# Crossbar transposes for two of four batches in a fused attention and gated-convolution kernel, with other first biases, smaller mask work and another instruction order

## The chip, the cores and the metric

One core of a Trainium2 chip runs the whole program. The metric is the device time of one execution in microseconds (us). The engines are called as in the profile: PE (matrix multiply), DVE (vector), ACT (scalar), POOL (GpSimd) and SP, which here only issues DMAs. PE writes its results to eight PSUM banks; DVE and ACT move them on to SBUF, the on-chip memory. All transfers, from whichever engine they are issued, run on the core's 16 DMA engines.

## The reference

Four batches, eight heads, 768 positions, head size 64. Each position attends to the 95 before it, itself and the first eight ("global") keys, with a penalty that grows with distance by a slope for each head. The attention output, 768 x 512 for each batch, goes through a gated long convolution:

```python
scores = scale * np.matmul(q, k.transpose(0, 1, 3, 2)) + bias      # bias = -slope * distance
a = softmax(np.where(keep, scores, -1e9))
x = np.matmul(a, v)                                  # to (batch, 768, 512)
x1, x2, x3 = np.split(x @ w_proj, 3, axis=-1)
x2_conv = np.fft.irfft(np.fft.rfft(x2, axis=1) * np.fft.rfft(filter_fft, axis=0), axis=1)
out = (x1 * x2_conv * x3) @ w_out
```

Inputs and output are float32; inside the kernel nearly everything is float16, with float32 sums in PSUM.

## The kernel before

**Attention** (`attention`, L855). Positions are taken in seven tiles of 120 keys, each with the eight global keys in front (128 rows), in three groups c0, c1, c2 of two, two and three tiles. For a group, q and k must stand transposed, head size on the partitions (`QT`, `KT`). There are three ways: `turned32` (L628) transposes float32 rows on PE, for the first tiles of batch 0, which SP loads as they are; `turned` (L665) transposes float16 tiles on PE, 4 matmuls of 128 columns a tile, and a copy on ACT or DVE moves them from PSUM; `crossed` (L651) has SP issue a DMA that transposes from SBUF to SBUF, without PE. The list `XB = (3,)` says that batch 3 goes the third way. Then, for each pair of heads hp and each group, `scores` (L685) multiplies k by q, ACT takes the exponential (L721), and DVE multiplies by a mask (L738), which holds the exponential of the distance bias and the zeros.

In batch 0 the masks are not ready in time, so there the bias is added on PE before the exponential: `slope` (a diagonal of the slope, in two halves of 64 rows) times `near` (the distances in two halves), L698, 96 matmuls in all. `near` and `slope` are written by ACT and DVE in `distances` (L477); `masks` (L535) spreads the distances into a row of 648 columns and takes eight exponentials of it on ACT, before batch 0's attention in the order of the program.

`values` (L741) multiplies the weights by v, divides by the sums (L780 on DVE, L784 on ACT), and leaves the attention output `xn` with positions on the partitions. `transpose_x` (L790) turns it on PE (L801) and ACT or DVE copies it to `xT` (L303), packed without gaps: 768 columns for each of four blocks of 128 features.

**Convolution** (`conv`, L891). `butterfly` (L808) adds and subtracts the two halves of `xT` on DVE; `gate` (L830) multiplies `xT` by the first and last third of the weights in two halves of 384 positions (L840) and multiplies the two results (L851); the projection (L909), the forward transform (L621), the product with the filter's spectrum (L1072 to L1078), the inverse transform (L934, L937) and the mixing on DVE follow, and `y` times the last weights gives the output rows (L961), six blocks of 128 a batch, stored by SP (L969) from a ring of six buffers `ot`. `tables` (L409) and `spectrum` (L549) make the transform's sines and the filter's spectrum once.

**The order.** `ORDER` (L39) is a list written out in the program: each word is an operation's number, the engine that runs it, and for PE the PSUM banks, as in `87P0`. Numbers count the operations in the order in which the program makes them. A word such as `i14b0` stands for 14 matmuls without use, which only keep PE busy. Each engine runs its operations in this order, so whichever is late holds up all behind it on its engine. Loads are issued by POOL (L319), which also converts to float16; SP issues the first float32 tiles, the copies of the global rows (`kn<-kn`, `vn<-vn`), the crossings and the stores. The costs in the program (`act`, `dve`, `pe`) were used to make such an order and do not run on the chip.

Of the kernel before, what the change touches and what calls it, by code (L numbers as in the profile page):

```python
# [26 lines left out]
def act(n):  # L27
    return 0.06 + n / 1200.0
# [11 lines left out]
5G 33V 34A 1V 16S 0V 12V 20S 4V 41A 43A 9V 8V 39A 10A 44A 36A 6A 49A 48A 19S 37A 45A 24G 17S 18S 50G 55G 25V 11V 26G  # L40
13V 56G 40A 42A 7V i14b0 87P0 54G 28A 53G 60G 31A 85P1 61G 59G 27A 72V 62G 52G 35A 81P2 51G 57G 46A 58G 83P3 47A 88A
29V 30V 32V 90P0 63G 89A 86A 82V 38A 91V 84A 21V 114P2 115V 94P01 98P45 116P2 78A 65G 99A 64G 15V 117V 95A 92P67 112P3
113V 93A 110P2 96P45 97A 158P3 66G 111V 122P01 123A 120P67 121A 22V 68G 159V 3G 160P3 161V 14V 23S 156P2 118P45 162P3
67G 119A 124P01 261G 157V 163V 164P23 125A 166P45 100P01 165A 101V 102V 167A 105P67 170P23 171A 69G 168P01 169A 131P45
262G 263G 106V 107V 108P2 132V 133V 260G 126P67 127V 76A 103P3 104A 109V 128V 75A 134P4 221P5 74A 135V 172P01 73A 173V
259G 129P6 216P4 177P23 79A 130V 136P6 174V 175P7 178V 70G 146P0 217A 264S 179V 180P1 137P2 222A 223V 142P3 176A 218V
219V 71G 80A 271G 202V 181A 183P1 182P4 203V 220A 224V 209V 144A 141P5 210V 138A 211V 148V 205V 361P3 273G 225A 139V
140V 272G 270G 265S 188P7 185A 362A 212V 213V 151P6 266G 363P3 2A 153V 143A 364V 359P2 360V 152P6 228P3 154V 276G
365P01 190A 184V 77A 204V 279G 366A 206V 207V 371P45 198P2 277G 226V 367V 155V 297P7 368P01 214V 372A 373V 215V 208V
200A 374P45 187P6 278G 229A 274G 145V 491G 298A 288P2 375A 269G 275G 369A 289A 488G 286P7 227V 235V 236V 189V 237V  # L50
147P4 149V 238V 287A 150V 230A 231A 232A 233V 284P2 285A 312P7 292P6 313A 293A 389P5 387P2 192P7 390A 194A 193P6 195A
388V 394P45 395A 400P01 234V 391P23 392A 239V 240V 376V 299P7 300A 437P6 401A 301P4 302A 282G 268S 433P5 435P7 438V
281G 370V 397P23 398A 241V 249P6 250A 393V 434V 247P4 436V 402V 267S 382P01 494S 242P5 248A 448P67 243A 439P23 493S
440A 383V 384V 449A 396V 303P4 377P01 197P5 199A 304A 399V 408P23 441V 492G 244P6 378V 379V 305P5 409V 410V 380P4
445P01 245A 442P23 280G 381V 306A 196V 446A 450V 403P67 404V 443A 411P5 489G 587P4 499G 405V 256P01 412A 490G 385P6
257A 505G 386A 258A 591P7 588V 252P45 253A 254A 507G 406P0 447V 456P23 661P1 444V 508G 501G 662A 407V 414P0 589P4 590A
251V 307V 416A 310P5 311A 511G 290P6 424P1 457V 458V 291A 426A 459P0 423P4 425A 429P6 308V 431A 500G 451P23 665P1
418P6 255V 592A 191V 615P4 314V 315V 506G 718G 309V 322P7 452V 246A 460A 502G 420A 453V 186V 323A 617P5 719G 454P0
455A 295V 294V 296V 732G 666V 318P6 721S 413P7 616A 330P0 316P2 509G 481V 482V 484V 317A 326P1 618A 415A 663P4 428P2
201V 430V 319A 320P3 321V 324P5 483V 325A 331V 328P7 327A 419P6 329A 421V 422V 495G 472P2 730G 664A 283G 734G 466P7  # L60
432V 476P3 474A 497S 468A 599P45 735G 628P01 478V 600A 498G 529P2 332V 629A 485V 486V 530A 462P3 676P45 677A 333V 601V
673P01 674A 596P67 487V 516P2 597A 334V 464A 512P4 726G 513A 527P5 602P67 517V 717G 593P23 603A 630V 728G 619P01 620A
525P4 675V 514P6 528V 335V 336V 339V 504G 526A 622P01 496S 594A 625P45 626A 340V 477P7 621V 623A 479A 627V 598V 515A
503G 737G 427V 467P2 469A 350P3 670P01 739G 624V 667P45 671A 540P7 541A 604V 353P6 722S 716G 533P2 668A 733G 595V 337V
461P0 354A 520P7 470V 531P1 605P45 417V 606V 521A 729G 351A 818S 538P6 607V 534A 356P7 539A 817S 636P45 338V 463A 637V
532A 638V 631P23 632V 357A 633A 518P0 471P1 639P7 640A 519A 672V 473A 669V 678V 341P6 342A 888S 610P45 608P2 344P3
345A 542V 611V 612V 510G 684P45 890S 609V 480V 613P2 634P6 614A 536V 465V 523V 679P01 635A 685V 686A 347P7 535V 646P6
652P2 654A 656P3 731G 843S 680V 681V 543V 648A 682P4 736G 658A 475V 687P5 688A 651P2 815S 522V 524V 653A 544P3 552P6
545A 537V 720G 816S 819S 823P01 824A 683V 553A 709V 710V 723G 724S 725S 712V 829P45 554P3 711V 713V 555A 647P2 830A
738G 714V 657P0 659A 548P3 549A 556P6 715V 546P1 547A 845S 660V 558P4 559A 649A 557V 704P0 706V 550P1 348A 551A 642P3  # L70
644A 560V 561V 690P2 692A 844S 727G 842S 562V 849P67 852P01 846P45 641P3 563V 564V 740P2 853A 753P0 847A 741V 826P45
850A 643A 855P67 820P23 754A 827A 744P1 891S 831V 567V 565V 699P0 821A 757P4 745A 568V 742P1 856A 655V 758A 566V 889S
854V 895P67 701A 768P4 743A 755P5 857V 746P1 352S 756V 896A 769A 747A 748P0 645V 355S 898P67 828V 901P45 892P23 575P1
825V 899A 749A 851V 650V 902A 848V 705P6 707A 822V 897V 689P0 900V 837P45 349S 838V 839V 893A 751V 700P6 702A 576A
695P7 697A 858P23 859V 860V 832P45 894V 766P1 767A 691A 759P7 761P6 762A 903V 578P1 750V 343S 752V 840P6 833V 863P23
864V 865V 760A 694P7 834V 579A 909P01 910V 911V 841A 346S 770V 904P23 861P6 862A 866P4 771V 572P5 573A 835P6 569P0
836A 912P5 905V 906V 584P6 763V 570A 764V 765V 867A 772P0 773A 907P4 784P1 908A 913V 934V 935V 780P2 778P0 696A 779A
781A 884P3 774P7 786P0 580S 936V 886A 708V 787A 937V 782P2 938V 358S 585V 581P3 785A 577S 776P1 775A 883P7 777A 783A
788V 958P0 959V 939V 940V 879P2 941P6 698V 586S 942V 789A 790V 885A 873P0 791V 881A 954P1 955A 875A 956P2 693V 967P1
969P6 957A 945P0 868P2 703V 930P7 968A 870A 943P1 960P2 962P4 869P5 792V 795V 796V 944A 961A 812P2 793V 970A 794V 946A  # L80
947P6 871A 574S 963A 971V 972V 887V 949P5 878P4 813A 950A 948A 874P2 876A 582A 803P5 964V 965V 966V 992P2 979P6 952V
951V 988P3 583S 975P0 980A 877V 800P1 953V 990P6 976A 880V 993A 804V 986P2 801V 991V 987A 989A 814S 994V 872V 977P4
978A 882V 973P5 974A 981V 995A 571S 996V 997V 982V 983V 984V 915P0 985V 809P6 797P1 810A 920P6 922A 998V 798A 999V
811S 1000V 1001V 919P5 932A 929P4 806P1 1012V 799S 917A 914P0 1002V 807A 808S 925P7 921A 923V 931A 933V 916V 927A 805S
918V 1013V 924P5 1009P4 926A 802S 1003P5 1004A 1005S 1014V 1010A 1011S 1006P0 1007A 1008S 928V 1015V 1019P5 1020A
1021S 1022P4 1023A 1016P5 1024S 1017A 1018S
# [112 lines left out]
class Fused:  # L199
    PERIOD = 40.0  # L200
    NEAR = 3
# [6 lines left out]
    XB = (3,)  # L208
# [26 lines left out]
    def buffers(self):  # L235
# [14 lines left out]
        self.xT = t("xT", [P, 4, S])  # L250
# [20 lines left out]
        self.x1p = t("x1", [P, 4, S // 2])  # L271
# [6 lines left out]
        self.dg = t("dg", [P, 264], BF16)  # L278
        self.far = t("far", [NG, 216])
        spare = self.eo.rearrange("p a b c -> p (a b c)")  # L280
        self.near = spare[:, 0:960].bitcast(BF16).rearrange("p (a b) -> p a b", a=2)
        self.slope = spare[:, 960:1984].bitcast(BF16).rearrange("p (a b c) -> p a b c", a=4, b=2)
        self.idle = t("idle", [P, 512])
        self.ident = t("ident", [P, P])
        self.ident32 = self.p3.bitcast(F32).rearrange("p a b -> p (a b)")[:, 256:384]
        self.warm = t("warm", [1, 2], F32)
        self.row = spare[0:1, 1984:2624].rearrange("p (a b) -> p a b", a=5)
        self.wide_dg = self.mix.bitcast(BF16).rearrange("p a b c -> p (a b c)")[:, 0:648]
# [76 lines left out]
    def setup(self):  # L365
# [12 lines left out]

        def rows(_):
# [10 lines left out]
        g.op("V", dve(512, 2), lambda _: v.memset(self.ot[3][0:NG], 0.0), w=[("kz", 0)], bias=-4500)  # L390
        for lo, hi in ((1, 2), (2, 7)):
            g.op("V", dve(512 * (hi - lo), 4), lambda _, lo=lo, hi=hi: v.memset(self.kn[0:NG, lo:hi], 0.0),
                 w=[("kz", t) for t in range(lo, hi)], bias=-4500 if lo == 1 else -3500)
# [15 lines left out]
    def tables(self):  # L409
# [3 lines left out]
        for a, n in enumerate((512, 256)):  # L413
# [16 lines left out]
            e, self.twin.rearrange("p s a (b c) -> p (s a) b c", b=2),  # L430
            self.fwd[:, 4:6].rearrange("p s (a c) -> p (s a) c", a=2)[:, :, None].to_broadcast([P, 4, 2, 64])),
            r=[("fwd", 1)], w=["twin"], name="twin")
        g.op("V", dve(256, 4), lambda _: nc.vector.tensor_scalar(
            self.fwd[:, 6:8], self.fwd[:, 1:4:2], -1.0, None, op0=Alu.mult), r=[("fwd", 0)],
            w=[("fwd", 2)])

# [787 lines left out]
```

## Time and profile before

| | us |
|---|---|
| three timed runs | 179.90, 180.12, 178.73 (median 179.9) |
| span of the profiled execution | 176.2 (no other time of this execution is shown) |
| busy: PE, DVE, ACT, POOL | 163.8, 156.3, 148.7, 78.2 |
| last matmul ends, last store issued | 172.5, 173.6 |
| first exponential, first crossing | 12.45, 82.9 |

A busy time is the part of the span in which an engine has at least one instruction under way. Matmuls overlap, so a full PE is not PE at its peak; in the chain of work that ended last each matmul has only the time by which it moved the end. `bank<-xT,w` is the tile written and the tiles read; L840 is the line, and for helpers such as `copy` (L303), `times` (L307, L309) and `load` (L319) it is that of the helper. The granted clock of TensorE is 1.00 in all stages.

### The profile page before, as it was taken

How to read it: one execution, taken by the hardware profiler on the slowest of the kernel's cores; microseconds unless marked ns; L12 is line 12 of the kernel's file. 1: busy time of each engine (PE TensorE's matmuls, PEld its weight loads, DVE VectorE, ACT ScalarE, POOL GpSimd, SP SyncE). 2: the span in 40 equal slices, each digit the busy share in tenths (PEclk: the TensorE clock that was granted, in tenths of full speed). 3: DMA queues.
4: the chain of work that ended last, by engine and by line, in shares of the span. 5: the costliest groups of instructions: out<-in, count | busy, mean ns of one | idle time of the engine just before them, and what ended most of it. 6: DMA issues, size and time to landing. Idle time of an engine off the chain costs nothing.

```text
span 176.2 us, 4332 instructions
## 1 busy us (share of the span) xinstructions
PE 163.8 (93%) x1662; PEld 100.3 (57%) x1662; DVE 156.3 (89%) x339; ACT 148.7 (84%) x294; POOL 78.2 (44%) x99
## 2 busy tenths in 40 slices
PE   5989999689999999999899999999999999989981
PEld 2547976354655767654356767444676644556530
DVE  7685569869999999999999999999999999999960
ACT  6999998949999988889989999899856855957852
POOL 7999998828999468799950000000000000000000
PEclk9999999999999999999999999999999999999999
DMA  4999999999999989999999995400031030041564
GB/s 110 184 149 140 142 173 170 196 193 154 159 155 159 149 53 106 156 167 155 130 161 169 131 96 159 179 4 0 0 118 65 0 125 0 0 180 40 192 242 186
DMA packets 98188, 22.23 MB, mean 126 GB/s; under 512 B 90879, under 2 KB 95095, under 8 KB 98167
## 3 DMA queue, kind: packets, MB, share of 16 engines
q0 software_dynamic: 82992, 12.41, 98.6%
q1 hardware_dynamic: 15175, 9.54, 23.1%
q8 instruction: 13, 0.21, 0.5%
q14 instruction: 8, 0.07, 0.1%
HBM read 25.84 MB, written 6.29 MB: 182 GB/s over the span
## 4 chain that ended last, share of the span: by engine, by line
DVE 48%; PE 15%; POOL 11%; ACT 11%; issue 7%; DMA 6%; POOLq 0%; DVEq 0%; ACTq 0%; SPq 0%
DVE E L738 6%; PE bank L961 4%; DMA kn<-in_k_dram 4%; DVE xn L780 4%; DVE y L1041 4%; POOL vn L319 4%; DVE g L851 3%; DVE y L1036 3%; PE bank L840 3%; ACT E L721 3%; POOL kn L319 2%; DVE ab L309 2%; POOL qn L319 2%; ACT g L849 2%; DVE pp L1072 2%
## 5 line engine op out<-in xcount | busy, mean ns | idle before, releaser
L840 PE MATMUL bank<-xT,w 128*128 128x384 f16 x256 | 48.5, 326 | 0.2 <-DVE x L309 0.2
L721 ACT ACTIVATE E<-bank 128x864 f16<-128x864 f32 x48 | 40.7, 900 | 4.1 <-issue 2.2
L840 PEld LDWEIGHTS <-w 128*128 128x128 f16 x256 | 23.7, 98 | 16.1 <-issue 1.4
L319 POOL DMA_DIRECT2D kn<-in_k_dram x27 | 25.1, 935 | 6.3 <-DMA g<-in_moe_filter_fft_dram 2.7
L319 POOL DMA_DIRECT2D vn<-in_v_dram x28 | 25.5, 917 | 0.8 <-PE bank L761 0.8
L961 PE MATMUL bank<-wo,y 128*128 128x512 f16 x96 | 23.9, 379 | 1.1 <-DVE y L1041 1.1
L319 POOL DMA_DIRECT2D qn<-in_q_dram x21 | 18.9, 905 | 4.0 <-PE bank L621 3.9
L738 DVE TENSOR_TENSOR E<-E,mask 128x864 f16<-128x864 f16 x36 | 20.2, 599 | 0.0
L780 DVE TENSOR_TENSOR xn<-bank,rc 128x512 f16<-128x512 f32 (+1 forms) x22 | 16.9, 774 | 0.7
L756 PE MATMUL bank<-vn,E 128*128 128x65 f16 x224 | 15.5, 193 | 0.2 <-DVE xn L780 0.2
L307 ACT ACTIVATE ot<-bank 128x512 f32<-128x512 f32 x21 | 12.6, 620 | 3.7 <-PE bank L961 3.3
L756 PEld LDWEIGHTS <-E 128*128 128x128 f16 x224 | 14.0, 97 | 2.8 <-issue 0.8
L303 ACT CAST eo<-bank 128x384 f16<-128x384 f32 x28 | 12.3, 496 | 3.8 <-PE bank L937 3.7
L761 PE MATMUL bank<-vn,E 128*128 128x65 f16 x192 | 15.3, 193 | 0.0
L707 PE MATMUL bank<-QT,KT 64*128 64x216 f16 (+2 forms) x224 | 14.4, 241 | 0.8 <-DVE ab L309 0.3
L849 ACT CAST g<-bank 128x384 f16<-128x384 f32 x28 | 13.9, 502 | 1.5 <-PE bank L840 1.2
L961 PEld LDWEIGHTS <-y 128*128 128x128 f16 x96 | 8.8, 98 | 10.1 <-DVE y L1041 2.2
L303 ACT CAST X<-bank 128x512 f16<-128x512 f32 x24 | 13.6, 607 | 0.7 <-PE bank L621 0.7
L761 PEld LDWEIGHTS <-E 128*128 128x128 f16 x192 | 13.2, 97 | 1.0 <-issue 0.8
L307 ACT ACTIVATE x<-bank 128x384 f16<-128x384 f32 x23 | 11.4, 509 | 1.8 <-PE bank L840 1.0
L707 PEld LDWEIGHTS <-KT 64*128 64x128 f16 x224 | 8.3, 94 | 7.5 <-issue 4.6
L934 PE MATMUL bank<-inv,X 128*128 128x256 f16 x64 | 11.4, 273 | 1.1 <-DVE X L1078 1.1
(148 smaller groups left out, 348.3 us busy)
## 6 DMA issues: line engine op xcount, KB each, us to landing
out_dram<-ot SPq DMA_DIRECT2D x24, 256.0 KB
vn<-in_v_dram POOLq DMA_DIRECT2D x28, 120.0 KB, 5.6
kn<-in_k_dram POOLq DMA_DIRECT2D x27, 120.0 KB, 5.8
qn<-in_q_dram POOLq DMA_DIRECT2D x21, 128.0 KB, 5.9
w<-in_moe_w_proj_dram POOLq DMA_DIRECT2D x4, 256.0 KB, 6.8
ot<-in_q_dram SPq DMA_DIRECT2D x3, 256.0 KB
g<-in_moe_filter_fft_dram POOLq DMA_DIRECT2D x1, 768.0 KB, 11.4
w<-in_moe_w_proj_dram POOLq DMA_DIRECT2D x1, 512.0 KB, 8.7
```

The costliest lines, as they stand in the source:

```text
L303: {"A": nc.scalar.copy, "V": nc.vector.tensor_copy, "G": nc.gpsimd.tensor_copy}[e](out, in_)
L307: self.nc.scalar.mul(out, in_, c)
L319: return self.g.op(eng, 0.57 + 0.00035 * nbytes[0] if eng == "G" else 0.5, lambda _: e.dma_start(dst, src), w=w, r=r, nbytes=nbytes, name= ...
L707: nc.tensor.matmul(bs[hh].f32()[:, off:off + w], self.KT[hs, hp, P * m:P * m + P], self.QT[hs, hp, KL * m:KL * m + w], start=(off == 0 and ...
L721: g.op("A", act(864), lambda _: nc.scalar.activation(eo, bs[0].two()[:, :, 0:432].rearrange("p h (m w) -> p h m w", m=2), Act.Exp, scale=s ...
L738: g.op("V", dve(864, 2), lambda _: nc.vector.tensor_mul(eo, eo, mk), r=[("mask", 2 * hp), ("mask", 2 * hp + 1)], w=[("E", hp, gi)], name=" ...
L756: nc.tensor.matmul(o[:, n, hh], ef[:, at:at + P], vt[:, t, 2 * hp + hh, 0:D + 1], start=first, stop=(t == 0), skip_group_check=True)
L761: nc.tensor.matmul(o[:, n, hh], ef[:, at:at + P], vt[:, t - 1, 2 * hp + hh, 0:D + 1], start=False, stop=True, skip_group_check=True)
L780: nc.vector.tensor_mul(to, o[:, :, :, 0:D], rc.to_broadcast([P, 2, 2 * nt, D]))
L840: nc.tensor.matmul(bk.f32()[:, 0:h], self.w[:, c, o + P * j:o + P * j + P], self.xT[:, c, h * s:h * s + h], start=(c == 0), stop=(c == 3))
L849: first = g.op("AV", {"A": act(h), "V": 0.0005}, lambda e: nc.scalar.copy(x3, pts[1].f32()[:, 0:h]) if e == "A" else None, use=[pts[1]], w ...
L961: nc.tensor.matmul(bk.f32(), y[:, c, P * t:P * t + P], self.wo[:, c, :], start=(c == 0), stop=(c == 3))
```

## The change

- `XB = (2, 3)`: q and k of batch 2 are crossed by SP too, 13 more tiles.
- `XX = (2, 3)`: the attention output of batches 2 and 3 is transposed by SP's DMAs, one for each of two j, two blocks of heads i and three groups (two or three tiles of 128 x 128 each). `xT` for these batches is not packed: seven tiles of 128 columns of which 120 (48 in the last) are used. So the butterfly's sums and differences are three instructions each, the gates take 360 and 408 positions instead of 384 and 384, and the second has a matmul of 48 columns behind each of 360.
- Batch 0's bias is a product of a full identity (`identb`) with rows of `near` that hold the distances times the slope for each head, 36 matmuls; two of these rows' corrections stand in `edge`. `near` is written by eight DVE instructions; `slope` is gone. It is an operation of its own, ahead of the scores.
- The masks are made behind batch 0's attention: eight exponentials of 216 columns, the rest by products and copies on DVE.
- Batch 0's k1 and q3 are loaded as float32 by SP and go through `turned32`.
- The halving of two rows of the spectrum (`ends`) moves to the sine tables. The last block of output rows is computed and stored in two halves (`HALVES`).
- `DF` and `DI`, other ways for the transforms, are empty and not used.
- A new `ORDER`: among others the filter is loaded fourth by POOL instead of after all of batch 0 and the weights, w0 and w1 come after the first loads of batch 1, the sine tables and the filter's sums come before batch 0's first exponential or between these, three useless matmuls stand at the start instead of 14 and three ahead of the end. DVE has 315 operations instead of 312, ACT 243 instead of 269, PE 295 instead of 302, SP 95 instead of 55.

```diff
-    NEAR = 3
-    XB = (3,)
+    XB = (2, 3)
+    XX = (2, 3)
+    NEAR = True
+    HALVES = (5,)
...
+    def biased(self, hp, gi, bs):
...
+                if gi < 2:
+                    mm(o[:, 0:432].rearrange("p (m w) -> p m w", m=2), self.identb,
+                       n[:, None, :].to_broadcast([P, 2, 216]), start=True, **kw)
+                    if gi == 0:
+                        mm(o[:, 0:KL], self.identb, self.edge[:, 0:KL], start=False, **kw)
+                    continue
+                for at, lo, w in ((0, 0, 216), (216, 0, 168), (384, 72, 48)):
+                    mm(o[:, at:at + w], self.identb, n[:, lo:lo + w], start=(at == 0), **kw)
+                mm(o[:, 384:432], self.identb, self.edge[:, KL:168], start=False, **kw)
...
     def masks(self):
...
-            g.op("A", act(648), lambda _, h=h: nc.scalar.activation(
-                self.mask[:, h], wide, Act.Exp, scale=self.slopes[h]), r=["wide"],
+            g.op("A", act(n), lambda _, h=h: nc.scalar.activation(
+                mask[:, h, n:2 * n], self.dg, Act.Exp, scale=self.slopes[h]), r=["dg"],
...
     def transpose_x(self, j, c):
...
+        if self.b in self.XX:
+            for i in range(2):
+                g.op("S", 0.3 + 0.25 * len(ts), lambda _, i=i: nc.sync.dma_start_transpose(
+                    out=self.xTt[:, 2 * j + i, ts[0]:ts[-1] + 1],
+                    in_=self.xn[j][:, i, ts[0]:ts[-1] + 1].rearrange("p t h d -> p (t h d)")),
+                    r=[("xn", j, c)], w=[("xT", j, c, i)], nbytes=(32 * len(ts), 1024), name="crossx")
+            return
...
     def butterfly(self, js):
...
+                fn(to[:, :, :, 0:96], t[:, :, 0:3, 0:96], t[:, :, 3:6, 24:KL])
+                fn(to[:, :, :, 96:KL], t[:, :, 0:3, 96:KL], t[:, :, 4:7, 0:24])
+                fn(ab[:, x, :, 360:h], t[:, :, 3, 0:24], t[:, :, 6, 24:48])
...
     def gate(self, b, j, s):
...
+                    nc.tensor.matmul(bk.f32()[:, 0:360].rearrange("p (t r) -> p t r", t=3), w,
+                                     self.xTt[:, c, 3 * s:3 * s + 3, 0:KL], skip_group_check=True, **kw)
+                    if s:
+                        nc.tensor.matmul(bk.f32()[:, 360:408], w, self.xTt[:, c, 6, 0:48], start=False,
+                                         stop=(c == 3), skip_group_check=True)
```

More of the change, by code (lines that the diff above doesn't have):

```diff
@@ L507, in third @@
                                 channel_multiplier=-sgn, compare_op=Alu.is_ge, fill=1.0)
-        g.op("G", 0.65, third, r=["far"], w=["far"], name="far")
-        near = self.near
-        for half in range(2):
-            for k in range(2):
-                src, dst = dg[64 * k:64 * k + 64], near[64 * half:64 * half + 64, k]
-                def spread(e, src=src, dst=dst):
-                    self.copy(e, dst[:, 0:n], src[:, 0:n])
-                    self.copy(e, dst[:, n:2 * n + 48], src)
-                g.op("AV", {"A": act(216) + act(264), "V": 0.6}, spread,
-                     r=["dg"], w=[("near", half, k)], bias=-2900, name="near")
-            g.op("V", dve(216, 1), lambda _, half=half: v.tensor_scalar(
-                near[64 * half:64 * half + NG, 0, 0:n], far, HUGE - NL, -HUGE, op0=Alu.mult,
-                op1=Alu.add), r=["far"], w=[("near", half, 0)], bias=-2900, name="near")
@@ new lines, in biased, with run @@
+    def biased(self, hp, gi, bs):
+        g, mm = self.g, self.nc.tensor.matmul
+        def run(_):
+            for hh in range(2):
+                o, n = bs[hh].f32(), self.near[:, 2 * hp + hh]
+                kw = dict(stop=False, skip_group_check=True)
+                if gi < 2:
[7 more added lines that the diff above has]
+                mm(o[:, 384:432], self.identb, self.edge[:, KL:168], start=False, **kw)
+        g.op("P", 2 * pe(*((432, KL), (432,), (216, 168, 48, 48))[gi]), run, acq=bs, name="bias",
+             r=[("near", 2 * hp), ("near", 2 * hp + 1), "identb"] + [[("edge", 0)], [], [("edge", 2)]][gi])
@@ L641, in turned32 @@
             w=[(what.upper() + "T", t)], name=what + "T")
-        if what == "k":
+        if what == "k" and t == 0:
             self.global_keys()
@@ L688, in scores @@
         m0 = self.GRP[gi]
+        if near:
+            self.biased(hp, gi, bs)
         def run(_):
             off = 0
-            if near:
-                runs = ([(0, 432)], [(216, 216), (216, 216)], [(216, 216), (216, 168), (432, 48)])[gi]
-                for at, w in runs:
-                    for k in range(2):
-                        for hh in range(2):
-                            hs = slice(64 * hh, 64 * hh + 64)
-                            nc.tensor.matmul(bs[hh].f32()[:, off:off + w], self.slope[hs, hp, k],
-                                             self.near[hs, k, at:at + w], start=(off == 0 and k == 0),
-                                             stop=False, skip_group_check=True)
-                    off += w
-                off = 0
             for m in m0:
@@ L871, in attention @@
                     self.turned32("k", 3, 0)
+                    self.turned32("k", 4, 1)
+                    continue
+                if b == 0 and c == 1 and what == "q":
+                    self.turned32("q", 5, 3)
                     ts = ts[1:]
@@ L875, in attention @@
             for i in range(4):
[L876 removed]
+                self.scores(i, c, self.NEAR and b == 0)
             for j in range(2):
@@ L1042, in gated @@
                                                                     gt[:, js, hs]),
-             r=ys + [("g", b % 2, j, half) for j in range(js.start, js.stop)], w=ys, name="y*g")
+             r=ys + [("g", b % 2, j, x) for j in range(js.start, js.stop) for x in ((0, 1) if half == 0 and b in self.XX else (half,))], w=ys, name="y*g")
     def spectra(self, b, pair):
@@ L1149, in graph @@
         g.batch = (-10.0, 0.0)
-        self.masks()
-        self.attention(0)
+        if self.NEAR:
+            self.biases()
+            self.attention(0)
+            g.batch = (-10.0, 0.0)
+            self.masks()
+        else:
+            self.masks()
+            self.attention(0)
         g.batch = (-10.0, 0.0)
         self.tables()
+        if self.DF:
+            self.dense_tables()
         g.batch = (0.0, self.PERIOD / 2)
         self.inverse_tables()
+        if self.DI:
+            self.dense_inverse()
         self.spectrum()
-        self.early = [x for x in g.ops if x.name in ("angles", "scores")]
+        self.early = [x for x in g.ops if x.name in ("angles", "scores", "bias", "mask0", "gaps")]
         for b in range(self.B):
```

424 lines of the change are left out of this document (266 added, 158 removed).

## The prediction

> **What bounds the kernel now.** First the page: its busy times, its slices and its chain.
>
> ```profile
> PE 163.8 (93%) x1662; PEld 100.3 (57%) x1662; DVE 156.3 (89%) x339; ACT 148.7 (84%) x294; POOL 78.2 (44%) x99
> ...
> PE   5989999689999999999899999999999999989981
> ...
> DVE  7685569869999999999999999999999999999960
> ACT  6999998949999988889989999899856855957852
> ...
> DMA  4999999999999989999999995400031030041564
> ...
> DVE 48%; PE 15%; POOL 11%; ACT 11%; issue 7%; DMA 6%; POOLq 0%; DVEq 0%; ACTq 0%; SPq 0%
> ```
>
> Three engines are nearly full from 36 us on and the DMA engines until 106 us. The chain names DVE for half the span, but PE is hardly freer. The chain in order of time gives PE's true spacing, which the mean duration of a matmul hides:
>
> ```profile
> 58.63 0.45 PE bank L672 x8
> ...
> 61.93 0.65 PE bank L840 x4
> ...
> 89.32 0.86 PE bank L961 x4
> ...
> 99.25 0.45 PE bank L801 x8
> ```
>
> So a transpose costs 0.056, a matmul of 384 columns 0.163, one of 512 0.215; on the same chain the 65-column ones of L756 and L761 stand 0.03 apart. Counting every matmul so, PE has 148 us of work besides the warm-ups. The trace has done 20 of it at 31.2 us, 30 at 44.0, 80 at 98.6, 140 at 162.1: from 44 us on 1.07 us per us of work, 1.00 in the best ten (120.4 to 130.4). Then the stages (PE, PEld, DVE, ACT, POOL busy):
>
> ```profile
> 23.00:36.00 13.00, 10.57 (x127) 6.85 (x124) 10.59 (x25) 12.46 (x23) 11.11 (x13) 1.00 1.68 183
> 36.00:50.00 14.00, 14.00 (x124) 8.11 (x123) 13.17 (x29) 11.76 (x22) 10.83 (x12) 1.00 2.18 165
> ...
> 125.00:140.00 15.00, 14.52 (x188) 10.41 (x187) 14.59 (x28) 10.54 (x23) 0.00 (x0) 1.00 0.14 54
> ```
>
> Only before 36 us is there room on PE and DVE; it waits for loads. Last the DMA queue that issues the transposes, SP's timeline:
>
> ```profile
> 85.44 4.78 SPq L660 DMA_TRANSPOSE QT<-qn  x2
> ...
> 104.03 2.52 SPq L660 DMA_TRANSPOSE KT<-kn  x2
> ```
>
> With nothing before it a transposed tile holds SP for 1.26 us.
>
> **Span and time.** The profiled execution shows a span of 176.2 and no other time. The timed runs are 178.73 to 180.12, median 179.9, so 3.7 lies around the span. The sum goes against 176.2, then 3.7 is added.
>
> **The change: PE.** Gone: 2 x 28 transposes of the attention output at 0.056 (3.1) and batch 2's 13 tiles of 4 (2.9). The biases: the 96 half-row matmuls of L698 keep PE about 0.36 for each of 12 groups (four of 432 columns show as 0.54, some 0.18 of it latency), 4.4 in all. The 36 full-row ones have 11,712 columns, at 512 in 0.215 4.9: +0.5. Two more f32 tiles through L634, where 12 matmuls take 1.47, against f16 ones: +0.4. The crossed gates split 360 and 408 as 360, 360 and 48 columns; 64 short matmuls at 0.03 instead of 0.02: +0.6. Sum -4.5, so 144 remain (warm-ups aside).
>
> **ACT and DVE.** ACT loses 16 slope writes (3.7), eight 648-column masks (5.6, against 3.0 for 216 columns by the 216-column copies at 0.371), the spreads (2.3), evacuations of batch 2's queries and keys (four of 1,024 at 1.03, two of 0.59) and of xT for two batches (nine, some 5.5), and one of three table loads (1.28). DVE loses 1.5 for the wide spread, 1.5 for far and slope, 1.1 and 1.2 of those evacuations, and 1.1 of the ends; it gains eight bias rows at about 0.2, four mask products at 0.37, two mask copies (0.7), 0.7 of small ones, and the split halves of the butterfly. That split is not in the trace: three pieces instead of one of 1536 at 0.95. From below nothing (the same elements), from above the rate of an f32 PSUM source, 0.95 per 768, so +0.95 each of four; I take 0.25, nearest to three starts. With the new order's choice of engine the durations sum to 166 instead of 175 on DVE and 162 instead of 172 on ACT; busy time is 0.87 of such sums, so about -8 and -9. Both fall by more than PE, so PE's pace can come nearer its best: I take 1.04.
>
> **DMA.** Between 40 and 45 us the trace moves 1,180 packets of loads per us, so a tile of 960 rows costs 0.80 of the DMA engines, a query tile 0.85; the filter's 768 rows cost 3.95 (195 per us at 33 to 37 us), w slices 1.55, and w4 2.6. A crossed tile is 512 packets. In the us from 89 on 510 of these ran beside 619 load packets, where 1,250 load packets move in the us after: 0.52 each, the lower bound; the upper one, 0.91, is under the rivals. The change adds 13 such tiles (6.8) and 24 transposes of the attention output (56 blocks, four to a tile: 7.3), 14 in all, of which about 11 lie before the last load. In these units the trace has landed 25 at 30.1 us, 45 at 50.7, 75 at 87.9: time is 1.04 u + 4 (with a 3.9 us wait of POOL for a buffer at 59 us in it). POOL needs 0.92 to issue what the engines move in 0.80, so SP's transposes may fill what POOL leaves: at best u + 4.
>
> **Start.** POOL issues k3, k2, k5 and then the filter ahead of q4, q5, k6, k4 and all values; 3.95 of DMA go before these. So the first exps start about as now (12.45), as q0 to q3, k0, k1 come by SP; the last four end two us later than their 22.8. That is covered: b1's k0 goes out seven issues earlier relative to the values, and its copy by SP (30.89 to 33.5, now on the chain) comes earlier. The sine tables and spectrum sums move into this room, so DVE has 5 us less to do later. The masks come behind the first attention; they are due only at the products of batch 1, and if late they delay those DVE products. The gate weights slip: w0 is the 33.9th unit (now 17.8th). PE's order puts 26.6 of work ahead of the gate that needs it, so at 37.9 (u + 4) PE has done 26.6; now it has about 25.
>
> **Path.** From there 117.4 remain at 1.04: 122.1. With the 3.7 after the last matmul as now (the last row halved saves at most 0.3, not counted), that makes 163.7. But PE's order is fixed, so a late load stops everything behind it. By u + 4: w4 (unit 41.9, for the first projection, 5.2 of work on) is 2.6 late; v6 of batch 1 (54.8, 9.6 on) 2.9; the transposed k4 of batch 2 (69.5, 14.5 on, and 2.5 us from issue through SP to landing, by the 2.9 us after 82.9 until packets moved) 2.1; q3 of batch 3 (89.5, 18 on) 1.3. Sum 8.9: 172.6, and 176.3 with the 3.7. SP's own order: about 26 x 1.3 and 24 transposes of two or three blocks at half to three quarters of it, 0.65 to 0.95, some 53 us between 45 and 125. A crossing that waits for its tile holds the next crossings and the copies of the global rows, so scores and values; store rows of batch 0 stand behind the output's crossings, and only the sixth later ot needs them. The output's crossing takes some 2.5 to 4 us where transpose and evacuation took 1; PE has 11 us of other work between the last values of batch 3 and its projection (gates, six outs of batch 1, eight inverses). Without that cover up to 3 per batch would show.
>
> **Clock.** The 14 warm-ups take 5.83, 0.43 apart, where 512 columns later take 0.215: PE runs at half pace until about 7.1 us. Only three stay ahead of the first work. From below 0, as loads pace this stage; from above 2.5, half of the some 5 us of PE work ahead of the first exp. I take 0 and keep 2.5.
> [...]
>
> **The rivals.**
> - *The loads keep pace*: no load late, 163.7 + 3.7 = 167.4; with half of the lateness 171.8. For it: DVE and ACT relief, POOL's gaps (3.87 at 59 us). Against: the DMA slices read 9 nearly everywhere.
> - *Nothing changes*: loads stay at 1.04 u + 4. Then w0 is at 39 and the four are 3.2, 3.4, 2.7 and 2.1 late: 39 + 122.1 + 11.4 + 3.7 = 176.2, thus 179.9. What the engines save, the crossbar takes.
> - *The slow start* alone: 178.8.
> - *Slower*: a crossing among loads costs more than 0.52. From 85 to 95 us 1,584 crossing packets (3.1 tiles) went with 9,040 load packets where 12,600 would have moved: 2.8 us lost, 0.91 each. Some 24 tiles lie ahead of the crossed q3 of batch 3, the last load that PE waits for: 24 x 0.39 = 9.4, so 172.6 + 9.4 + 3.7 = 185.7. It decides from 0.67 each on, where 24 x 0.15 = 3.6 is lost. For it: that mean, and SP's 4.78 for two. Against: half of the loss falls in 86 to 88 us, in one stall; in the clear second at 89 the price is 0.52, which I keep for that reason.
>
> **How the numbers follow.** The forecast, 176.3, 0.35; loads keep pace 0.15; nothing changes 0.15; slow start 0.05; slower 0.30. Runs of this kernel differ by 0.8%, so about 1% can be told. Faster by over 1% (below 178.1): 0.35 + 0.15 = 0.50. Within: 0.15 + 0.05 = 0.20. Slower (over 181.7): 0.30. The range goes from 171.0, with half of the first rival below it, to 185.0, with a good third of the slower one above it. The forecast's own range is 174 to 178.
>
> **What would show it.** Right: L801 at 56, L672 down by 52, DVE near 148 and ACT near 139 busy; PE idle named by DMA at w4, v6 of batch 1 and the crossings of batches 2 and 3; the DMA slices at 9 until 105 us or later. Wrong: PE waits for xT's crossings (cover too thin), 30 us of PE work reached after 44 us (start slower than now), first f32 transposes twice as far apart (clock), DMA idle before 95 us with PE never waiting for it (loads keep pace), or DVE still without idle time at 60 to 120 us, which would make DVE and not the loads the bound.

## The result, and the profile after

The changed kernel takes 198.24 us (median of four runs, 196.55 to 199.45), the kernel before 179.31 beside it (178.02 to 180.12): 1.105 times as long, 95% interval 1.096 to 1.114. The forecast was 176.3, in a range of 171 to 185. The profiled execution has a span of 197.3 us, against 176.2. Here and below a time is the median of all runs of a kernel, while a ratio compares only the runs in the faster of the chip's two states, so the two do not always divide out.

The same lines of the page as before, with the granted clock:

```profile
PE 165.0 (84%) x1574; PEld 101.5 (51%) x1574; DVE 148.0 (75%) x333; ACT 140.0 (71%) x280; POOL 75.8 (38%) x95
...
PE   5956997999996970699489917998999899999993
...
DVE  7814696999986890169539970779999979999961
ACT  7960998899897870459638914796978876969651
...
PEclk9999999999999996579969985999999999999999
DMA  4999999999999999999999996235151260402355
...
DMA 43%; PE 39%; POOL 5%; DVE 3%; SPq 3%; issue 2%; ACT 2%; DVEq 0%; POOLq 0%
```

DVE and ACT have become lighter by as much as forecast, and the end shows nothing of it: in slice 16 (74 to 79 us) PE, DVE and ACT are empty together, and in slices 17, 20, 21, 24 and 25 (79 to 84, 94 to 104 and 113 to 123 us) at least one of the three is at 4 or less, while the DMA engines stay at 9 until slice 24 (118 us; before until 106). The chain, half DVE before, is now DMA for 43%. In order of time it is one long wait:

```profile
53.74 12.81 DMA kn<-in_k_dram
...
68.62 16.65 DMA wo<-in_moe_w_out_dram
...
85.56 11.05 DMA qn<-in_q_dram
...
98.90 13.54 DMA qn<-in_q_dram
...
112.46 7.12 DMA QT<-qn
```

The last two rows are q3 of batch 3: its load lands at 112.4, its crossing at 119.6, and only then does PE go on. By stages (PE, PEld, DVE, ACT, POOL busy, clock, DMA share, GB/s):

```profile
65.00:80.00 15.00, 7.87 (x85) 4.86 (x83) 9.38 (x15) 7.48 (x13) 8.13 (x10) 0.85 1.94 143
110.00:125.00 15.00, 9.26 (x91) 5.08 (x89) 7.25 (x17) 7.30 (x15) 0.00 (x0) 0.77 1.26 113
125.00:140.00 15.00, 14.37 (x143) 9.46 (x142) 13.54 (x29) 12.97 (x29) 0.00 (x0) 1.00 0.34 95
```

PE is busy for 52% and 62% of the first two and nearly full in the third. Counted by the spacings of the prediction, PE reaches 50 us of its work at 70.5 us (before 65.4), 80 at 125.4 (98.7), and from there on it keeps pace (140 at 186.9; 162.2). So 5 us are lost by 50 units and some 21 more by 80.

The transfers between 56 and 97 us, first before, then after:

```profile
DMA packets 39208, 5.71 MB, mean 139 GB/s; under 512 B 38573, under 2 KB 39203, under 8 KB 39203
...
q0 software_dynamic: 36247, 4.82, 181.1%
q1 hardware_dynamic: 2956, 0.83, 14.2%
```

```profile
DMA packets 33114, 5.52 MB, mean 135 GB/s; under 512 B 32473, under 2 KB 33112, under 8 KB 33112
...
q0 software_dynamic: 25337, 3.50, 164.8%
q1 hardware_dynamic: 7775, 1.99, 53.3%
```

The bytes moved are nearly the same. What SP's transfers (q1, of which the crossings are the part that grew) took, 1.16 MB more, the loads (q0) got less, 1.32 MB.

### The profile page after: what moved, and what is told of

It reads as the page before. It is cut to its first block, busy times and chain, and to the rows that moved or that the text cites. A ratio compares the mean times of both kernels' runs of the same rounds, so it can differ in the third digit from the quotient of the medians.

```text
span 197.3 us, 4233 instructions
## 1 busy us (share of the span) xinstructions
PE 165.0 (84%) x1574; PEld 101.5 (51%) x1574; DVE 148.0 (75%) x333; ACT 140.0 (71%) x280; POOL 75.8 (38%) x95
## 4 chain that ended last, share of the span: by engine, by line
DMA 43%; PE 39%; POOL 5%; DVE 3%; SPq 3%; issue 2%; ACT 2%; DVEq 0%; POOLq 0%
DMA qn<-in_q_dram 12%; PE bank L1079 9%; DMA wo<-in_moe_w_out_dram 8%; PE bank L940 8%; DMA kn<-in_k_dram 6%; DMA ot<-in_k_dram 6%; PE bank L1017 5%; DMA w<-in_moe_w_proj_dram 4%; DMA QT<-qn 4%; PE bank L1045 3%; POOL vn L329 3%; DMA xT<-xn 2%; POOL kn L329 2%; PE bank L708 2%; SPq L329 2%
## 5 line engine op out<-in xcount | busy, mean ns | idle before, releaser
L797 ACT ACTIVATE E<-bank 128x864 f16<-128x864 f32 x48 | 41.0, 897 | 22.4 <-PE bank L785 21.4
L329 POOL DMA_DIRECT2D vn<-in_v_dram x28 | 25.6, 914 | 14.6 <-DMA kn<-in_k_dram 4.7
L329 POOL DMA_DIRECT2D kn<-in_k_dram x26 | 24.0, 926 | 9.6 <-DMA KT<-kn 2.6
L938 PE MATMUL bank<-xT,w 128*128 128x384 f16 x128 | 25.6, 335 | 0.3 <-DVE KT L313 0.3
L940 PE MATMUL bank<-xT,w 128*128 128x360 f16 x128 | 23.3, 314 | 1.3 <-DMA xT<-xn 0.7
L1079 PE MATMUL bank<-wo,y 128*128 128x512 f16 (+1 forms) x100 | 24.2, 387 | 0.0
L329 POOL DMA_DIRECT2D qn<-in_q_dram x20 | 17.9, 900 | 6.6 <-DMA wo<-in_moe_w_out_dram 1.8
L785 PEld LDWEIGHTS <-KT 64*128 64x128 f16 x224 | 8.8, 98 | 20.5 <-issue 10.3
L833 PEld LDWEIGHTS <-E 128*128 128x128 f16 x224 | 14.2, 98 | 7.8 <-issue 4.0
L862 DVE RECIPROCAL rc<-bank 128x8 f32<-128x8 f32 (+1 forms) x24 | 5.1, 211 | 17.4 <-PE bank L838 17.2
L317 ACT ACTIVATE x<-bank 128x384 f16<-128x384 f32 (+2 forms) x29 | 14.1, 508 | 4.0 <-PE bank L938 2.2
L317 ACT ACTIVATE ab<-bank 128x512 f16<-128x512 f32 x24 | 14.4, 617 | 2.5 <-PE bank L1017 2.4
L857 DVE TENSOR_TENSOR xn<-bank,rc 128x512 f16<-128x512 f32 (+1 forms) x20 | 15.5, 780 | 0.4
L838 PE MATMUL bank<-vn,E 128*128 128x65 f16 x192 | 15.5, 194 | 0.0
L313 ACT CAST eo<-bank 128x384 f16<-128x384 f32 x26 | 11.2, 492 | 5.3 <-PE bank L1048 5.2
## 6 DMA issues: line engine op xcount, KB each, us to landing
vn<-in_v_dram POOLq DMA_DIRECT2D x28, 120.0 KB, 10.4
```

What stands on the lines that cost most here:

```text
L313: {"A": nc.scalar.copy, "V": nc.vector.tensor_copy, "G": nc.gpsimd.tensor_copy}[e](out, in_)
L317: self.nc.scalar.mul(out, in_, c)
L329: return self.g.op(eng, 0.57 + 0.00035 * nbytes[0] if eng == "G" else 0.5, lambda _: e.dma_start(dst, src), w=w, r=r, nbytes=nbytes, name= ...
L785: nc.tensor.matmul(bs[hh].f32()[:, off:off + w], self.KT[hs, hp, P * m:P * m + P], self.QT[hs, hp, KL * m:KL * m + w], start=(off == 0 and ...
L797: g.op("A", act(864), lambda _: nc.scalar.activation(eo, bs[0].two()[:, :, 0:432].rearrange("p h (m w) -> p h m w", m=2), Act.Exp, scale=s ...
L833: nc.tensor.matmul(o[:, n, hh], ef[:, at:at + P], vt[:, t, 2 * hp + hh, 0:D + 1], start=first, stop=(t == 0), skip_group_check=True)
```

## The experiments

In the texts below, three theories compete at first: a high *price* of a crossing, its *latency* alone, and the new *order* as such.

**Parts of the change undone.** Three kernels put turns on PE back into the kernel after, one puts batch 2's crossings into the kernel before. In `ORDER` the turns stand where the crossings stood, in the first PSUM bank that is free.

```diff
-    XB = (2, 3)          # a_qk2_pe and c_both_pe
+    XB = (3,)
-    XX = (2, 3)          # b_out_pe and c_both_pe
+    XX = ()
...
-    XB = (3,)            # d_before_qk2, in the kernel before
+    XB = (2, 3)
```

> The kernel after, with the 13 query and key tiles of batch 2 turned on TensorE again (batch 3's and both batches' attention output stay with the crossbar; every other operation keeps its place in the order). The price theory: each crossed tile keeps the load flow for about 1.28 us, where the prediction took 0.52, so 13 x 1.28 = 16.6 us of the wait for loads go and 13 x 4 turns at 0.056 us = 2.9 us of TensorE come: 181 to 187 us. The latency theory (a crossing costs the flow 0.52 us and is only slow to land): 6.8 us go and 2.9 come, 192 to 196. The order theory (the loss comes from the order in which loads and work are issued, not from the crossings): 197 to 201.

Measured: 196.24 us, 1.096 (1.087 to 1.105) times the kernel before.

> The kernel after, with the attention output of batches 2 and 3 turned on TensorE again (the query and key tiles of both batches stay with the crossbar). The price theory: the 28 blocks of batch 2, seven tiles' worth, lie among the loads and give back 7 x 1.28 = 9.0 us, TensorE gets 3.1 us, of which the half lies in the loads' stretch: 190 to 194 us. The latency theory: 3.6 us go and 3.1 come, 196 to 199. The order theory: 198 to 201.

Measured: 205.85 us, 1.141 (1.128 to 1.154).

> The kernel after, with batch 2's query and key tiles and both batches' attention output on TensorE again, so that the biases, the masks and the new order are what is left of the change. The price theory: 20 x 1.28 = 26 us of load flow come back, more than the 21 us lost between 58 and 125 us, and the 5 us lost at the start stay: 178 to 185 us. The latency theory: 188 to 192. The order theory: 197 or more.

Measured: 199.72 us, 1.118 (1.110 to 1.126).

> The kernel before, with one thing changed: the 13 query and key tiles of batch 2 go through the crossbar, where their turns stood in the order. The price theory: 13 x 1.28 = 16.6 us more of load flow, less the few us by which loads are early in places and less 2.9 us of TensorE: 187 to 193 us. The latency theory (0.52 a tile): 180 to 184. The order theory (a crossing costs nothing, the order does): 177 to 180.

Measured: 184.00 us, 1.029 (1.019 to 1.039).

The price theory missed all four, the first three by 9 to 15 us too low, the fourth by 3 too high. The order theory had the third, missed the first by 0.8 and the other two by 4 or more. The latency theory had the fourth and missed the first by 0.2. But these kernels change more than was meant. POOL's waits in the third and in the first show it (total, times, longest):

```profile
POOL kn L346 <- PE bank L776: 9.5, 3, 5.6
POOL vn L346 <- PE bank L902: 5.4, 1, 5.4
```

```profile
POOL kn L346 <- PE bank L776: 10.2, 3, 5.6
POOL vn L346 <- PE bank L902: 7.7, 1, 7.7
```

L776 and L902 are the turns put back. The next loads wait for the buffers that these read, and each turn waits in PE's fixed order. An order made for crossings is not fit for turns, so these kernels do not price a crossing. The second, `b_out_pe`, shows no such wait and is still the slowest. As the table below counts, it has as many crossed tiles ahead of its last load as the kernel after, 25.8: nearly all of the crossings that it takes out stand behind that load. So it could not test their price among the loads, and what its turns cost behind the last load (85.4 us instead of 78.5) was not taken apart. In the fourth, POOL waits 10.3 and 6.1 us for the crossings of `qn` and `kn` to have read their buffers: a cost of a crossing beside its share of the flow.

**The price by itself.** Two kernels without any computation:

```python
for i in range(96): load(i)                       # POOL; the second kernel: 48 loads of 512 rows of 1 KB
for i, n, times in [(12, 4, 12), (40, 2, 12), (64, 3, 12), (95, 4, 12)]:
    for _ in range(times): cross(i, n)            # SP: n blocks of tile i, once it has landed
```

> A kernel with all computation left out: GpSimd issues 96 loads of 1,024 rows into buffers of their own, with no wait but its ring; SyncE issues twelve four-block crossings once load 12 has landed, twelve two-block ones after load 40, twelve three-block ones after load 64, and twelve four-block ones after the last load; then the output is stored as zeros. The price theory: each four-block crossing among the loads takes 1.2 to 1.35 us of their flow (12 of them: some 15 us in which only what the engines move besides gets through), and if what it keeps them for is the crossing itself and not its bytes, two and three blocks cost about the same. The latency theory: 0.5 us for four blocks, 0.25 for two. Alone, after the last load, the price theory has twelve in 14 to 16 us, since SyncE holds each for as long; the latency theory has them in 6 to 8.

> As the one with row loads, but with 48 loads of 512 rows of 1 KB (256 columns of the projection weights), for which GpSimd's issue is no bound, and with the crossings at the same shares of them. The price theory: 1.2 to 1.35 us of flow per crossing, whatever the size of the load's rows; a theory in which the row size decides (short packets of the crossing taking turns with long ones of the loads) has a different price here, more than 1.6 us.

Of the first kernel, the stretches without a crossing, with two-block ones, with four-block ones, and with four-block ones alone (POOL busy, clock, DMA share, GB/s):

```profile
40.00:50.00 10.00, 0.00 (x0) 9.38 (x11) 1.00 2.43 155
52.00:64.00 12.00, 0.00 (x0) 10.21 (x13) 1.00 2.14 156
...
28.00:36.00 8.00, 0.00 (x0) 4.38 (x5) 1.00 1.73 156
112.00:124.00 12.00, 0.00 (x0) 0.00 (x0) 1.00 0.49 98
```

The engines move 155 GB/s with crossings or without. (The profile counts a load's row by the 128 B that are written as float16, 1.55 MB for 12,262 rows; 256 B are read for it, 25.17 MB for all 98,304.) A crossing takes its bytes out of that: 128 KB at 155 GB/s is 0.84 us. By packets it is the same: the loads move 12,262 in 10 us free of crossings and 4,315 in the 8 us from 28 to 36; the 5,494 that are missing are 4.48 us of flow, for 0.70 MB of crossings or 5.34 tiles, 0.84 each. Two blocks cost 0.41. Among rows of 1 KB, without and with four-block crossings:

```profile
9.00:13.00 4.00, 0.00 (x0) 2.23 (x3) 1.00 1.45 196
24.00:36.00 12.00, 0.00 (x0) 4.44 (x6) 1.00 1.36 184
```

There the total falls, and a four-block crossing costs 0.81. By its bytes at the 196 GB/s of these loads it would be 0.67, so the price is not set by the rate of the loads beside it: it is 0.20 to 0.21 us a block in both kernels, neither 0.52 a tile nor SP's hold of 1.25 us. For twelve two-block crossings among loads, and for twelve four-block ones alone, SP needs the same time, so its hold does not follow the size:

```profile
50.31 15.37 SPq L45 DMA_TRANSPOSE T<-L  x12
...
110.02 15.58 SPq L45 DMA_TRANSPOSE T<-L  x12
```

**The same order, with the crossings cheaper.** Now nothing is put in their place.

```diff
-        x = g.op("S", 0.5, lambda _: nc.sync.dma_start_transpose(out=o, in_=i), nbytes=(128 * n, 1024),
+        x = g.op("S", 0.5, lambda _, b=self.b: None if b == 2 else nc.sync.dma_start_transpose(
+            out=o, in_=i), nbytes=(128 * n, 1024),                                   # x_qk_none, x_none
...
+        x = g.op("S", 0.5, lambda _, b=self.b: nc.sync.dma_start_transpose(out=o[:, 0] if b == 2 else o,
+            in_=i[:, 0:P] if b == 2 else i), nbytes=(128 * n, 1024),                 # x_one
...
-                    out=self.xTt[:, 2 * j + i, ts[0]:ts[-1] + 1],                     # x_one; none at all in x_none
-                    in_=self.xn[j][:, i, ts[0]:ts[-1] + 1].rearrange("p t h d -> p (t h d)")),
+                    out=self.xTt[:, 2 * j + i, ts[0]],
+                    in_=self.xn[j][:, i, ts[0]].rearrange("p h d -> p (h d)")),
```

and, in the fourth, `52G` (the filter's load) moved behind `43G` in `ORDER`.

> The kernel after in its own order, with the 13 crossings of batch 2's queries and keys and the 24 of both batches' attention output left out and nothing in their place (TensorE reads what the buffers hold from before, so the later batches' result is that of stale data; every other instruction stays). The flow theory: with the 0.84 us per four-block crossing that the kernel of loads alone showed, the 20 tiles' worth that lie ahead of the last load give back 17 us, the last load lands at about 102 us instead of 119, and, with 71 us of TensorE's work behind it as in both kernels, the end comes at 179 to 184 us. The order theory (the new order makes the loads late by itself, as the three kernels with turns put back suggest): the last load stays at 112 us or later, and the time at 190 us or more.

Measured: 181.59 us, 1.013 (1.003 to 1.023).

> The kernel after, with each of those 37 crossings cut to one block of 128 x 128 (the rest of its target keeps old data): the same instructions, the same hold of SyncE, the same waits before and behind each, and a third of the blocks. The flow theory by blocks (0.21 us each, from the kernel of loads alone): about 55 blocks fewer ahead of the last load, 11.5 us back: 185 to 189 us. A theory by instructions (each crossing stops the flow for as long as SyncE holds it, 1.25 us, whatever its size): 196 to 200. The buffer theory (a crossing's late read of its source keeps the buffer from the next load): 196 or a little less.

Measured: 185.98 us, 1.043 (1.033 to 1.053).

> The kernel after, with batch 2's 13 crossings of queries and keys left out and the attention output still crossed (that batch's scores are of stale data). The flow theory: 13 x 0.84 = 10.9 us back: 185 to 190 us. The order theory: 195 or more.

Measured: 183.21 us, 1.025 (1.017 to 1.032).

> The kernel after, with the load of the filter put four loads later in GpSimd's order, behind the query tiles 4 and 5 and the key tile 6 of batch 0. The flow theory: the first tiles of SyncE land some 2 us earlier, the first exponentials start 2 us earlier, and the end stays within 1.5 us, 196.5 to 200, because the last load, not TensorE's start, sets it. A start theory (the 5 us lost before the first exponentials are handed on to the end): 193 to 196.

Measured: 196.24 us (195.96 to 199.19), 1.097 (1.088 to 1.107).

The flow theory named the first two and was 2 us too high for the third. In the first two that was luck, as the table below shows: it had counted 20 tiles fewer ahead of the last load, and 55 blocks fewer in the second, where 12.9 tiles and 39 blocks (9.7 tiles) are fewer. What stands is that the order theory falls with the first and the third, and the theory by instructions with the second: the same 37 instructions with a third of the blocks give 12 us back. The fourth lies between its two theories. Its first exponential starts at 16.29 us instead of 19.85, PE reaches 40 units at 57.5 instead of 58.0, and the last load lands 2.7 us earlier; that, not the start, is what the end shows. (By the medians it is 2.0 us, and the four runs of the kernel after alone differ by 2.9, so it is not clear of noise.) All kernels in one table, each by its profiled execution; a tile is four blocks, counted by its 512 packets of 256 B after 25 us:

| kernel | span | last row load moves | crossed tiles ahead of it | last load less 0.84 a tile | span behind it |
|---|---|---|---|---|---|
| before | 176.2 | 96.6 | 4.5 | 92.8 | 79.6 |
| after | 197.3 | 118.8 | 25.8 | 97.1 | 78.5 |
| s_filter | 194.6 | 116.1 | 25.9 | 94.4 | 78.5 |
| x_one | 182.9 | 106.3 | 16.1 | 92.8 | 76.5 |
| x_qk_none | 181.5 | 103.3 | 13.4 | 92.1 | 78.2 |
| x_none | 179.8 | 102.9 | 12.9 | 92.1 | 76.9 |
| d_before_qk2 | 181.6 | 108.4 | 17.3 | 93.9 | 73.2 |
| a_qk2_pe | 195.4 | 112.9 | 9.9 | 104.6 | 82.4 |
| b_out_pe | 201.2 | 115.8 | 25.8 | 94.2 | 85.4 |
| c_both_pe | 198.1 | 111.4 | 10.9 | 102.2 | 86.7 |
| g_before_c0 (below) | 180.8 | 97.2 | 2.9 | 94.8 | 83.6 |
| g_before_out3 (below) | 184.4 | 99.3 | 5.9 | 94.3 | 85.1 |

In the order of the kernel after, with nothing put on PE in the crossings' place (rows two to six), the last load lands at 92 to 97 us plus 0.84 for each crossed tile ahead of it, and the end comes 76.5 to 78.5 behind it. Of the 22.2 us by which the last load is later than before, 21.3 tiles explain 17.9.

The 5 us between 92 and 97 go with the crossings too. Against the kernel after, `x_qk_none`, `x_none` and `x_one` have 12.4, 12.9 and 9.7 tiles fewer ahead of the last load, and it comes 15.5, 15.9 and 12.5 us earlier: 1.23 to 1.29 us a tile (1.21 to 1.29 by the medians of the times), with order and filter as they were. In the order of before, 12.8 tiles more cost 0.92 each (`d_before_qk2`). So 0.84 is what a crossing takes of the flow, and in the kernel after each took some 0.4 more; what that is was not tried apart. The crossings of the attention output have little part in it: with batch 2's queries and keys already left out, leaving them out too (`x_none` against `x_qk_none`) gives 1.6 us.

**Two attempts at a better kernel.** Both in the order of the kernel before: fewer crossings ahead of the last load, or more behind it.

```diff
-                if b in self.XB:
+                if b in self.XB and (b, c) not in self.PEC:       # g_before_c0; PEC = ((3, 0),)
...
+    XX = (3,)                                                     # g_before_out3, with transpose_x as after
```

> The kernel before, with the first five query and key tiles of batch 3 (q0 to q2, k0, k1) turned on TensorE again, so that fewer of its 13 crossings lie ahead of the last load. The flow theory in the form that the runs so far give (the last load lands at 92.8 us plus 0.84 us for each crossed tile ahead of it, and the end comes 77 to 80 us behind it): before has 4.5 tiles ahead of it, and up to 3.8 us come back, against 1.1 us of turns on TensorE: 175 to 178 us. A theory in which VectorE's chain behind the last load sets the end by itself: 178 to 181.

Measured: 182.04 us, 1.018 (1.012 to 1.024), above both theories. Only 1.6 tiles fewer are ahead of the last load, which does not move, so the rule is not tried downward by this. The end comes 4 us later behind it, where the five turns with their copies stand: from 100 to 115 us PE is busy 13.1 us and DVE 12.6, where before has 14.7 and 14.6.

> The kernel before, with the attention output of batch 3 alone through the crossbar (12 crossings, all behind the last load, where no load pays for them; the gate reads the tiles at their wider spacing in five pieces). The flow theory: the loads do not move; TensorE is spared 28 turns (1.6 us) and VectorE and ScalarE six evacuations (some 3 us), and each crossing lands later than a turn and its evacuation would: 176 to 180 us. A theory by instructions, in which a crossing holds up everything behind it wherever it stands: 12 x 1.25 = 15 us in SyncE's queue, of which part shows: 183 or more.

Measured: 187.26 us, 1.046 (1.039 to 1.053). Here the time comes from SP's hold for each instruction, which the loads did not show. No load pays, but the crossings stand on the chain:

```profile
136.44 0.64 SPq L797
137.13 1.25 SPq L797
138.48 1.19 SPq L797
140.13 1.18 SPq L797
141.42 1.19 SPq L797
142.66 2.38 DMA xT<-xn
```

SP issues one in 1.2 us and the last takes 2.4 more, 8.6 us in all. Before had turns and copies there, with no such queue: its butterfly starts at 137.9 us, this one at 145.2, which is 7.3 of the 8.2 us of span lost. No kernel tried is faster than the one before.

## Why the prediction was wrong

**Right: the engines' work.** DVE is busy 148.0 and ACT 140.0, forecast near 148 and 139. The output's turns (L801, now L885) are 56, the other turns (L672, now L759) 80 instead of 140: 52 fewer, and 8 for the two tiles that came to `turned32`. It was also right that loads set the time and that PE would wait at crossings.

**Right: what lies behind the last load.** The forecast had 172.6 for the span with q3 of batch 3 crossed at 93.5 + 2.5 = 96.0, so 76.6 us behind it. Measured are 197.3 and 119.6: 77.7. Of the span's error of 24.7 us, 23.6 are the time at which this one tile lands: its load comes 19.0 us late, at 112.5 instead of 93.5, and its crossing 4.6.

**Wrong: "0.52 each, the lower bound".** This is the step on which the forecast failed. A crossed tile costs 0.84 of the load flow by the kernel of loads alone, and 1.23 to 1.29 us by leaving crossings out in place. The prediction read it in one us at 89, where 510 crossing packets went with 619 load packets (by its own counts 0.51). Over ten us the same rows gave 0.91, which it set aside as the effect of one stall. The longer mean was nearer. For the 24 tiles ahead of q3: 24 x 0.32 = 7.7 us by the flow, 24 x 0.73 = 17.5 by the price in place.

**Wrong: "at best u + 4".** The forecast let SP's crossings fill what POOL's slow issue (0.92 for 0.80 of flow) left. In the kernel without computation the same issue keeps the engines at 149 and 152 GB/s in the two slices from 7.3 to 14.5 us, ahead of the first crossing, and with crossings beside the loads they move 155 to 156: there was next to nothing to fill. With 1.04 u, the pace that the prediction read from before, the some 90 units of q3 come 3.6 us later. That pace itself does not fit its third row: 75 units at 87.9 us lie 5.9 above 1.04 u + 4, and POOL's wait for a buffer is 3.9 of them.

**Wrong: 2.5 us from issue to landing.** That holds alone. Among the loads of the kernel without computation the median is 6.3 to 7.2 us, and q3's crossing shows 7.12 on the chain: 4.6 more.

**Wrong: the start.** The first exponential starts at 19.85 us, not at 12.45. Its last tile is k1, which SP issues at 4.69:

```profile
4.69 11.58 DMA ot<-in_k_dram
```

It lands at 16.3, behind three key tiles and the filter, which POOL issued by 4.95. The prediction counted these loads against POOL's later ones, not against SP's first tiles. By `s_filter` the early filter costs the last load 2.7 us, if it is not noise; the start itself, covered by the loads, shows no further cost at the end.

**Wrong, outside the sum: SP's hold.** The prediction gave crossings of two and three blocks 0.65 to 0.95 us of SP; they take 1.2 to 1.3. On the chain behind the last load this shows twice, each time with a landing of 2.3 to 2.4 us behind it (128.8 to 133.1 and 152.5 to 155.2 us). The full-row bias matmuls are 56 in the trace, not 36; their columns, by which they were priced, were right.

Together 7.7 + 3.6 + 4.6 + 2.7 = 18.6 of 23.6 us, of which only the 7.7 and the 4.6 have a measurement of their own. The 3.6 and the 2.7 are no costs of the new order by itself: `x_none` has the same issue and the same early filter, and its last load less its tiles stands at 92.1, where before has 92.8. Counted by the price in place, 17.5 + 4.6 = 22.1 of 23.6 us go with the crossings. **Open** is why that price is 0.4 above the flow's. The flow is weaker than 155 GB/s in each kernel here: from 56 to 97 us it is 135 in the mean after, 139 before, 144 in `x_none` and 148 in `x_one`. `wo` takes 16.7 us to land after and 8.3 in `x_none` and `x_one`. What holds the flow there (the issue waiting for earlier transfers, buffers that are given back late) was not tried apart.

**The rivals.** *Slower* had the right mechanism and nearly the right price (0.91), and still gave 185.7, since it kept u + 4 and 2.5. *The slow start* was there: the four float32 transposes of a tile take 1.1 us, where before twelve take 1.47, and a bias row of 432 columns has 0.36 until 19 us and some 0.22 from 22 us on. Nothing of it shows at the end, because the loads covered it. From 16.4 us on PE works without a long wait, and by 21.4 us the spacing of these rows has halved (0.46 us from one to the next at 17.3 us, 0.24 at 21.4). The granted clock reads 1.00 from 16 to 25 us, so only the spacing shows it; what sets the wide one was not tried. Later the granted clock falls: it is 0.85 from 65 to 80 us, where PE waits 4.5 us for `KT`, 0.81 and 0.89 in the two stages of 15 us behind that, and 0.77 from 110 to 125, where PE waits 5.7 us for `QT`. That costs the end nothing that shows: behind the last load PE's 70 us of work take 78.5, and before 71 take 79.6.

## What to carry to other kernels

Work that is moved to the DMA engines is not free: beside loads it takes from them, and where the engines are idle the hold of its queue can stand on the chain, as in `g_before_out3` (1.2 us each). Price it by what it was measured to take from the loads beside it (here 0.81 to 0.84 us for 128 KB), expect more in place (here 1.2 to 1.3), count what lies ahead of the last load that the program waits for, in the order in which it is issued, and add the end's distance behind that load. Read a contention price from a mean over many such transfers, or measure it with a kernel of transfers alone, rather than from the one us that looks cleanest. When a run lands in a theory's range, check that the counts in the theory were right too. An order written for one way of doing a step does not serve another, so putting a step back in the same order does not price it; leaving it out or making it smaller in place does.

## What the runs showed of the hardware

- A crossing costs the flow by its blocks (0.84 us for four, 0.41 for two, among rows of 256 B; 0.81 for four among rows of 1 KB), but holds its issuing queue by the instruction: twelve of two blocks for 15.37 us, twelve of four for 15.58, those of two or three on the chain of `g_before_out3` for 1.18 to 1.25 each. Alone, four-block ones reach 98 GB/s.
- The same engines that move 155 GB/s of 256 B rows move 382 GB/s when the output is stored in rows of 2 KB at the end of that kernel. In bytes as written, a crossing goes as fast as the loads of 256 B rows beside it (0.84 us for 128 KB, 155 GB/s); among rows of 1 KB, 0.81 us for 128 KB is 162 GB/s against the loads' 196.
- Time from issue to landing of a crossing: 2.5 us alone, 6.3 to 7.2 among row loads, 10.4 among rows of 1 KB.
